# P·V matmuls of an attention kernel issued as three pairs in every third step instead of one pair in each

## The chip, the cores and the metric

The kernel runs on one core of a Trainium2 chip. Its engines work side by side, each with a queue of its own in program order: TensorE (PE, with its weight loader PEld), VectorE (DVE), ScalarE (ACT), GpSimd (POOL), and SyncE (SP), which only issues transfers. The metric is the device time of one execution in microseconds (us); the kernel before takes 831.34 us, the median of three runs (831.29 to 833.1).

## The reference

Attention with a hashing mask (a query sees the keys of its own hash bucket), and two expert layers behind it. Cut to what is computed:

```python
q_bits = (einsum('bhsd,dk->bhsk', q, proj) > 0)          # k_bits likewise, 6 bits each
mask = q_bucket[:, :, :, None] == k_bucket[:, :, None, :]  # bucket = number made of the bits
scores = where(mask, q @ k.T / sqrt(64), -1e9)
attn = exp(scores - max(scores)); attn = attn / (attn.sum(-1) + 1e-9)
x = attn @ v                                              # heads side by side: 1536 x 512
h = x @ w_in;  x = (h - tanh(h)) @ w_out                  # 512 -> 2048 -> 512
out = (silu(x @ w_gate) * (x @ w_val)) @ w_out2           # 512 -> 1536 -> 512
```

Batch 2, 8 heads, sequence 768, head size 64; activations are float32, the weights come as float64.

## The kernel before, in words

**Stages.** The attention stage runs to about 265 us, the two expert layers from there to the end. The order of all instructions on all queues is the order in which the Python code emits them.

**Steps.** The heads are taken in pairs (8 pairs over both batches). A pair has 12 steps: 2 halves of the queries (384 each) × 2 heads `e` × 3 query tiles of 128. That makes 96 steps. The loop at line 529 emits, in iteration `i`:

- `emit_qk(i)` (line 276): the scores of step i, four matmuls into the PSUM tile `s` (two buffers);
- `emit_t(i - 3)` (line 310): six transposes of the probabilities of step i − 3 into the PSUM tile `t`, of which there is one buffer (`ps_t`, line 65), and the copy of `t` into `pt` by ACT (line 323);
- the P·V part (lines 534 to 539), below;
- matmuls that prepare the next pair of heads (`pe[i]`): `hash_mm` at offset 0 of the pair's 12 steps, one one-hot matmul (line 189) at offsets 2, 4, 6 and 8;
- `emit_soft(i)` (line 290): the row maximum `m` on DVE, then the exponential on ACT, which reads `s` and writes `p`;
- `emit_norm(i - 1)` (line 301): two small operations on DVE, then the multiplication of `p` by the reciprocal on POOL;
- other preparation for the next pair (`late + ot[i]`): compares and splits on DVE, ACT (line 204, at offsets 2 to 5) and POOL, and transfers. In the last pair of heads, which has no next one, the first weight chunks are converted instead (three DVE operations, lines 96, 102 and 107, one in each step).

**P·V.** `emit_pv(n, half, kt)` (line 321) issues one pair: for both heads of the pair the matmul of V's 128 keys `kt` (64 columns wide, each head in its own half of the array's columns) with the transposed probabilities. Six pairs, `kt` 0 to 5, add up to one PSUM tile `x`; after the sixth ACT copies it to `xh` (line 345), and the operation `xl` on DVE (line 346) is put into `late`. When the last transposes of a half are emitted, its six pairs join the list `pv` one iteration later (line 537), at i = 9, 15, 21, ... The loop then takes one of them per iteration. Iterations 96 to 107 have no scores; there the expert layers' first matmuls (`a1_mm`, line 358) are emitted too.

Of the kernel before, what the change touches and what calls it, by code (L numbers as in the profile page):

```python
# [30 lines left out]
LAG = 3  # L31
WA, WB = 6, 8
PRE = 6


def chunk_keys():
# [19 lines left out]
def lsh_attention_moe_kernel(ctx: ExitStack, tc: tile.TileContext, qT, kT, vP, proj, cst, wts, out):  # L56
# [25 lines left out]
    def load_next():  # L82
        if n_load[0] < len(keys):
            raw = raw_p.tile([128, 512], I64, tag="raw", name="raw")
            nc.sync.dma_start(out=raw, in_=wts[n_load[0]])
            raws[n_load[0]] = raw
            n_load[0] += 1

    def conv_op(c, step):
        """One of the three integer operations that turn float64 bits into float32 bits."""  # L90
        w = raws[c].bitcast(U32).rearrange("p (n t) -> p n t", t=2)
        lo32, hi32 = w[:, :, 0], w[:, :, 1]
        if step == 0:
            f = raw_p.tile([128, 512], U32, tag="f", name="f")
            cw[c] = f
            nc.vector.tensor_scalar(  # L96
                out=f, in0=hi32, scalar1=3, scalar2=0x3FFFFFF8,
                op0=ALU.logical_shift_left, op1=ALU.bitwise_and,
            )
        elif step == 1:  # L100
            f = cw[c]
            nc.vector.scalar_tensor_tensor(  # L102
                out=f, in0=lo32, scalar=29, in1=f, op0=ALU.logical_shift_right, op1=ALU.bitwise_or
            )
        else:
            f = cw[c]
            nc.vector.scalar_tensor_tensor(  # L107
                out=f, in0=hi32, scalar=0xC0000000, in1=f, op0=ALU.bitwise_and, op1=ALU.bitwise_or
            )
            raws.pop(c)  # L110
            load_next()

    def conv_split(c):
        pool, tag = (wa, "wa") if c % (WA + WB) < WA else (pool_b[0], "wb")
        dst = pool.tile([128, 2, 512], F32R, tag=tag, name=tag)
        ff = cw.pop(c).bitcast(F32)
        nc.scalar.activation(out=dst[:, 0, :], in_=ff, func=ACTF.Copy)
        nc.gpsimd.tensor_tensor(out=dst[:, 1, :], in0=ff, in1=dst[:, 0, :].bitcast(F32), op=ALU.subtract)  # L118
        wgt[keys[c]] = dst

    def conv_slot():
        """One stage of the weights' conversion: split the chunk before, convert the next."""
        if n_split[0] < n_conv[0]:
            conv_split(n_split[0])
            n_split[0] += 1
        if n_conv[0] < len(keys) and live[0] < WA + WB:
            for step in range(3):
                conv_op(n_conv[0], step)
            n_conv[0] += 1
            live[0] += 1  # L130
# [3 lines left out]
    with tc.manual_schedule():  # L134
        nc.scalar.dma_start(out=pj, in_=proj)

        with ExitStack() as at:
# [8 lines left out]
            yin, vin, ldin, bits = {}, {}, {}, {}  # L146
            aq, bq, ak, bk = {}, {}, {}, {}

            def load_y(n):
                t = y_p.tile([128, 2, S], F32, tag="y", name="y")  # L150
                nc.sync.dma_start(out=t[:, 0, :], in_=qT[n * 128:(n + 1) * 128, :])
                nc.sync.dma_start(out=t[:, 1, :], in_=kT[n * 128:(n + 1) * 128, :])
                yin[n] = t
# [6 lines left out]
            def load_h(n, src, nm, eng=nc.sync, heads=(0, 1)):  # L160
                for e in heads:
                    r0 = (2 * n + e) * 64
                    t = ld_p.tile([128, S], F32, tag=nm, name=nm)
                    eng.dma_start(out=t[0:64, :], in_=src[r0:r0 + 64, :])
                    eng.dma_start(out=t[64:128, :], in_=src[r0:r0 + 64, :])
                    ldin[n, e, nm] = t
# [78 lines left out]
            ot = {k: [] for k in range(-12, 12 * len(pairs) + 24)}  # L245

            def prep(n):
                """The pair's preparation, by step: PE work and other work."""
                def put(d, k, f, *a):
                    d[12 * (n - 1) + k].append(lambda: f(n, *a))  # L250

                put(pe, 0, hash_mm)
                put(ot, 1, hash_bits)
                for i, (side, half) in enumerate(((1, 0), (1, 1), (0, 0), (0, 1))):
                    put(pe, 2 + 2 * i, oh_mm, side, half)
                    for e in range(2):
                        put(ot, 2 + 2 * i + e, oh_cmp, side, half, e)
                for i, (e, half) in enumerate(((0, 0), (1, 0), (0, 1), (1, 1))):
                    put(ot, i, hi_a, e, half, "k")
                    put(ot, (4, 4, 5, 6)[i], k_lo, e, half)  # L260
                    put(ot, (5, 7, 9, 10)[i], hi_a, e, half, "q")
                    put(ot, (7, 8, 10, 11)[i], hi_b, e, half)
                    put(ot, (10, 11, 12, 14)[i], q_lo, e, half)
                if n + 1 < len(pairs):
                    put(ot, 0, lambda n: load_y(n + 1))
                    put(ot, 7, lambda n: load_h(n + 1, kT, "k"))
                    put(ot, 14, lambda n: load_h(n + 1, qT, "q"))
                put(ot, 8, load_v)
# [32 lines left out]
            def emit_norm(i):  # L301
                p, sm = pp[i], rr.pop(i)
                r = st_p.tile([128, 1], F32, tag="r", name="r")
                nc.vector.tensor_scalar(out=r, in0=sm, scalar1=1e-9, scalar2=None, op0=ALU.add)
                nc.vector.reciprocal(out=r, in_=r)  # L305
                nc.gpsimd.tensor_scalar(out=p, in0=p, scalar1=r, scalar2=1.0, op0=ALU.mult, op1=ALU.mult)  # L306
# [21 lines left out]
            def emit_pv(n, half, kt):  # L328
                if kt == 0:
                    pool, tag = (ps_h, "h") if (n, half) == (len(pairs) - 1, 1) else (ps_x, "x")  # L330
                    xps[0] = pool.tile([128, TB], F32, tag=tag, name="x")
                x = xps[0]
                for e in range(2):
                    r = slice(64 * e, 64 * e + 64)
                    nc.tensor.matmul(  # L335
                        out=x[r, :], lhsT=vin[n][:, kt, r], rhs=pt[n, half, e][:, kt, :],
                        start=(kt == 0), stop=(kt == NKT - 1), tile_position=(0, 64 * e),
                    )
                if kt == NKT - 1:
                    b, p = pairs[n]  # L340
                    tb = 2 * b + half
                    if p == 0:
                        xh[tb] = xp.tile([128, KT, TB], F32R, tag="xh", name="xh")
                        xl[tb] = xp.tile([128, KT, TB], F32R, tag="xl", name="xl")
                    nc.scalar.activation(out=xh[tb][:, p, :], in_=x, func=ACTF.Copy)
                    late.append(lambda: nc.vector.tensor_tensor(
                        out=xl[tb][:, p, :], in0=x, in1=xh[tb][:, p, :].bitcast(F32), op=ALU.subtract
                    ))
# [134 lines left out]
                f, *a = moe.pop(0)  # L483
                f(*a)

            # the first pair: what its first step needs comes first
            load_y(0)
            load_h(0, kT, "k", nc.scalar)
            load_h(0, qT, "q")
# [36 lines left out]
            pv = []  # L526
            nsteps = len(steps)
            conv0 = nsteps - 12
            for i in range(nsteps + 2 * PRE):
                if i < nsteps:  # L530
                    emit_qk(i)
                if LAG <= i < nsteps + LAG:
                    emit_t(i - LAG)
                if LAG < i <= nsteps + LAG:
                    n2, half2, e2, qt2 = steps[i - LAG - 1]
                    if e2 == 1 and qt2 == 2:
                        pv += [(n2, half2, kt) for kt in range(NKT)]
                if pv:
                    emit_pv(*pv.pop(0))
                for f in pe[i]:  # L540
                    f()
                if i < nsteps:
                    emit_soft(i)
                if 1 <= i <= nsteps:
                    emit_norm(i - 1)
                for f in late + ot[i]:
                    f()
                late.clear()
                c, step = divmod(i - conv0, 3)
                if 0 <= c < PRE:  # L550
                    if step == 0 and c:
                        conv_split(c - 1)
                    conv_op(c, step)
                elif c == PRE and step == 0:
                    conv_split(PRE - 1)
                if i == nsteps:
                    a1_mm(0, 0, 0)
                elif i == nsteps + LAG - 1:
                    emit_moe()
                elif i == nsteps + LAG:  # L560
                    a1_mm(0, 0, 1)
            assert not pv and not late
            n_conv[0] = n_split[0] = live[0] = PRE

# [64 lines left out]
```

## Time and profile before

| what | value |
|---|---|
| median of 3 runs | 831.34 us |
| span of the profiled execution, first to last instruction | 829.2 us |
| PE busy | 810.4 us, 98% of the span |
| PEld busy | 704.2 us, 85% |
| DVE, ACT, POOL busy | 495.0, 340.4, 401.8 us |
| granted TensorE clock, mean | 1.000 of full speed |

The page gives the profiled execution's span, not its whole time; the median of the runs lies 2.1 us above that span. Busy time of PE is the time in which at least one matmul is under way, with modelled ends. "Idle before" is the time an engine had nothing under way before an instruction, and the name behind the arrow is what ended it; "issue" means that nothing in the profile released it.

### The profile page before, as it was taken

To read this page: it belongs to the slowest core of one execution; us is meant where nothing else is said; L and a number is where in the kernel's file an instruction comes from. 1 tells how busy PE (TensorE), PEld (TensorE's weight loads), DVE (VectorE), ACT (ScalarE), POOL (GpSimd) and SP (SyncE) were. 2 spreads that over 40 slices of the span, in tenths; PEclk is the share of its full clock that TensorE was granted. 3 is DMA by queue.
4 is the path that set the end of the run, shared out by engine and by line. 5 is a ranking of instruction groups with operands and counts; after the bars stand their busy time and mean duration, and the time that the engine had idled before them with its cause. 6 is when DMAs were issued, how large, how long until landed. Compare 5 with 4: busy or idle time off the path is not lost.

```text
span 829.2 us, 11946 instructions
## 1 busy us (share of the span) xinstructions
PE 810.4 (98%) x4560; PEld 704.2 (85%) x4560; DVE 495.0 (60%) x807; ACT 340.4 (41%) x610; POOL 401.8 (48%) x404
## 2 busy tenths in 40 slices
PE   5999999999999999999999999999999999999998
PEld 2766666666667999999999998999999999999996
DVE  5777777777784885475376367246835663572222
ACT  2887887788783432232233134222312221221110
POOL 4766766666663773363165177334623441351110
PEclk9999999999999999999999999999999999999999
DMA  8533243231022331121022023002402120210012
GB/s 249 161 96 98 74 119 93 90 102 39 20 78 79 121 130 51 46 100 59 27 92 87 0 102 102 1 26 82 148 1 77 55 98 4 74 51 1 1 39 114
DMA packets 20344, 61.93 MB, mean 75 GB/s; under 512 B 2800, under 2 KB 2800, under 8 KB 20288
## 3 DMA queue, kind: packets, MB, share of 16 engines
q1 hardware_dynamic: 19712, 60.04, 22.0%
q10 hardware_dynamic: 464, 0.80, 0.4%
q8 instruction: 36, 0.59, 0.3%
q0 software_dynamic: 112, 0.33, 0.2%
q14 instruction: 20, 0.16, 0.1%
HBM read 58.02 MB, written 3.15 MB: 74 GB/s over the span
## 4 chain that ended last, share of the span: by engine, by line
PE 92%; DVE 3%; ACT 1%; issue 1%; DMA 1%; POOL 1%; ACTq 0%; POOLq 0%; DVEq 0%
PE pa L358 38%; PE pb L423 15%; PE pb L453 12%; PE s L282 9%; PE x L335 9%; PE t L318 7%; DMA k<-in_kT 1%; PE hps L189 1%; PE hps L174 1%; DVE f L102 1%; DVE f L96 0%; POOL glo L368 0%; DVE th L384 0%; DVE m L293 0%; POOL wb L118 0%
## 5 line engine op out<-in xcount | busy, mean ns | idle before, releaser
L368 POOL TENSOR_TENSOR glo<-u,ghi 128x384 fp32r<-128x384 f32 x48 | 52.8, 1099 | 179.2 <-ACT ghi L367 147.0
L306 POOL TENSOR_SCALAR p<-p,r 128x768 f32<-128x768 f32 x96 | 96.4, 1004 | 71.0 <-DVE r L305 39.8
L368 POOL TENSOR_TENSOR glo<-th,ghi 128x384 fp32r<-128x384 f32 x64 | 76.4, 1214 | 104.0 <-ACT ghi L367 104.0
L358 PE MATMUL pa<-x2h,wb 128*128 128x384 f32 x448 | 116.7, 335 | 1.9 <-DVE u L397 1.9
L293 DVE TENSOR_REDUCE m<-s 128x1 f32<-128x768 f32 x96 | 91.7, 955 | 34.8 <-PE s L282 33.5
L323 ACT ACTIVATE pt<-t 128x768 f32<-128x768 f32 x96 | 77.6, 808 | 43.8 <-PE t L318 42.9
L296 ACT ACTIVATE p<-s,m 128x768 f32<-128x768 f32 x96 | 86.2, 898 | 11.7 <-DVE m L293 9.1
L396 DVE TENSOR_TENSOR u<-pa,u 128x384 f32<-128x384 f32 x48 | 26.7, 556 | 106.1 <-ACT u L395 106.1
L358 PEld LDWEIGHTS pa<-x2h,wb 128*128 128x128 f32 x448 | 81.1, 188 | 2.5 <-DVE u L397 2.2
L358 PE MATMUL pa<-x2h,wa 128*128 128x384 f32 x320 | 83.2, 334 | 0.0
L335 PE MATMUL x<-pt,v 128*64 128x384 f32 x384 | 82.3, 510 | 0.0
L395 ACT ACTIVATE u<-pa 128x384 f32<-128x384 f32 x48 | 23.6, 492 | 139.0 <-PE pa L358 137.6
L318 PE MATMUL t<-csb,p 128*128 128x128 f32 x576 | 79.7, 275 | 0.9 <-ACT pt L323 0.7
L107 DVE SCALAR_TENSOR_TENSOR f<-raw,f 128x512 uint32<-128x512 uint32 x68 | 77.6, 1141 | 2.2
L318 PEld LDWEIGHTS t<-csb,p 128*128 128x128 f32 x576 | 69.1, 142 | 6.9 <-issue 2.5
L358 PE MATMUL pa<-x2l,wb 128*128 128x384 f32 x224 | 74.9, 334 | 0.0
L423 PE MATMUL pb<-ghi,wa 128*128 128x384 f32 x256 | 70.7, 334 | 0.0
L423 PE MATMUL pb<-ghi,wb 128*128 128x384 f32 x256 | 70.7, 334 | 0.0
L282 PEld LDWEIGHTS s<-aqk 128*128 128x128 f32 x192 | 31.3, 196 | 43.4 <-issue 27.3
L358 PE MATMUL pa<-xh,wa 128*128 128x384 f32 x256 | 66.9, 336 | 1.0 <-DVE th L384 1.0
L358 PE MATMUL pa<-xh,wb 128*128 128x384 f32 x256 | 66.2, 334 | 0.0
L282 PE MATMUL s<-aqk 128*128 128x384 f32 x192 | 62.2, 406 | 2.3 <-DVE aqk L232 1.5
(75 smaller groups left out, 1677.4 us busy)
## 6 DMA issues: line engine op xcount, KB each, us to landing
raw<-in_w SPq DMA_DIRECT2D x68, 512.0 KB, 3.2
q<-in_qT SPq DMA_DIRECT2D x32, 192.0 KB, 4.4
k<-in_kT SPq DMA_DIRECT2D x28, 192.0 KB, 3.2
y<-in_qT SPq DMA_DIRECT2D x8, 384.0 KB, 3.2
y<-in_kT SPq DMA_DIRECT2D x8, 384.0 KB, 4.5
v<-in_v SPq DMA_DIRECT2D x8, 384.0 KB, 3.2
out<-acc SPq DMA_DIRECT2D x4, 512.0 KB, 2.8
out<-acc SPq DMA_DIRECT2D x4, 256.0 KB, 2.0
```

Source lines behind the costliest of these rows:

```text
L107: nc.vector.scalar_tensor_tensor(out=f, in0=hi32, scalar=0xC0000000, in1=f, op0=ALU.bitwise_and, op1=ALU.bitwise_or)
L282: nc.tensor.matmul(out=s[:, kh, 0:TB], lhsT=a[n, e, half][:, q0], rhs=b_[n, e, kh], start=first, stop=not first,)
L293: nc.vector.tensor_reduce(out=m, in_=s, axis=AX.XY, op=ALU.max, negate=True)
L296: nc.scalar.activation(out=p.rearrange("p (a b) -> p a b", a=2), in_=s, func=ACTF.Exp, bias=m, accum_out=sm)
L306: nc.gpsimd.tensor_scalar(out=p, in0=p, scalar1=r, scalar2=1.0, op0=ALU.mult, op1=ALU.mult)
L318: nc.tensor.transpose(out=t[:, kt // 3, c0:c0 + 128], in_=p[:, kt * 128:(kt + 1) * 128], identity=ident)
L323: nc.scalar.activation(out=dst, in_=src, func=ACTF.Copy)
L335: nc.tensor.matmul(out=x[r, :], lhsT=vin[n][:, kt, r], rhs=pt[n, half, e][:, kt, :], start=(kt == 0), stop=(kt == NKT - 1), tile_position= ...
L358: nc.tensor.matmul(out=ps, lhsT=w[:, wi, kt * 128:(kt + 1) * 128], rhs=(xh, xl)[xi][tb][:, kt, :], start=(n == 0), stop=(n == 3 * KT - 1),)
L368: nc.gpsimd.tensor_tensor(out=lo, in0=src, in1=hi.bitcast(F32), op=ALU.subtract)
L423: nc.tensor.matmul(out=ps[:, d, 0:TB], lhsT=w[:, wi, dt * 128:(dt + 1) * 128], rhs=gt[xi], start=(n == 0), stop=(n == 3 * G1 - 1),)
L453: nc.tensor.matmul(out=ps[:, d, :], lhsT=u[xi][:, t], rhs=w[:, wi, :], start=(n == 0), stop=(n == 3 * G2 - 1),)
```

## The change

Iterations whose number is a multiple of 3 take up to three pairs from the list, the others none. Line numbers below the new constant are higher by one. (The diff also takes away comments.)

```diff
+PVB = 3
...
-                if pv:
-                    emit_pv(*pv.pop(0))
+                if i % PVB == 0:
+                    for _ in range(min(PVB, len(pv))):
+                        emit_pv(*pv.pop(0))
```

On PE, from the transposes of iteration 9 on, the instructions before stand so (`t` are transposes, `x` the P·V matmuls, `s` the scores):

```order
L318 MATMUL t<-csb,p 128x128 x6
L335 MATMUL x<-pt,v 64x384 x2
L282 MATMUL s<-aqk 128x384 x2
L282 MATMUL s<-bqk 128x384 x2
L318 MATMUL t<-csb,p 128x128 x6
L335 MATMUL x<-pt,v 64x384 x2
L282 MATMUL s<-aqk 128x384 x2
L282 MATMUL s<-bqk 128x384 x2
L318 MATMUL t<-csb,p 128x128 x6
L335 MATMUL x<-pt,v 64x384 x2
L282 MATMUL s<-aqk 128x384 x2
L282 MATMUL s<-bqk 128x384 x2
```

and after the change so:

```order
L319 MATMUL t<-csb,p 128x128 x6
L336 MATMUL x<-pt,v 64x384 x6
L283 MATMUL s<-aqk 128x384 x2
L283 MATMUL s<-bqk 128x384 x2
L319 MATMUL t<-csb,p 128x128 x6
L283 MATMUL s<-aqk 128x384 x2
L283 MATMUL s<-bqk 128x384 x2
L319 MATMUL t<-csb,p 128x128 x6
L283 MATMUL s<-aqk 128x384 x2
L283 MATMUL s<-bqk 128x384 x2
L319 MATMUL t<-csb,p 128x128 x6
L336 MATMUL x<-pt,v 64x384 x6
```

The two matmuls of a pair that stood between the transposes and the next scores in each step are now six in one step, and in the next two steps scores follow directly on transposes.

On ACT, from the copy of iteration 12 on, there stand before (`p` is the exponential, `xh` the first half of the P·V result, `bqk` preparation):

```order
L323 ACTIVATE pt<-t 128x6x128
L296 ACTIVATE p,sm<-s,m 128x768
L323 ACTIVATE pt<-t 128x6x128
L296 ACTIVATE p,sm<-s,m 128x768
L323 ACTIVATE pt<-t 128x6x128
L345 ACTIVATE xh<-x 128x384
L296 ACTIVATE p,sm<-s,m 128x768
L204 ACTIVATE bqk<-hps,csb 64x384
```

and after:

```order
L324 ACTIVATE pt<-t 128x6x128
L346 ACTIVATE xh<-x 128x384
L297 ACTIVATE p,sm<-s,m 128x768
L324 ACTIVATE pt<-t 128x6x128
L297 ACTIVATE p,sm<-s,m 128x768
L324 ACTIVATE pt<-t 128x6x128
L297 ACTIVATE p,sm<-s,m 128x768
L205 ACTIVATE bqk<-hps,csb 64x384
```

`xh` has moved two steps forward, from iteration 14 (offset 2) to iteration 12 (offset 0), in front of that iteration's exponential; the rest keeps its order. In the second half of a pair of heads it moves from offset 8 to offset 6 in the same way.

## Rows read from the trace of the kernel before

**Rows 1.** From the windows view: one stretch of the attention stage, 36 to 218 us. Columns: the stretch, its length, busy us (and number of instructions) of PE, PEld, DVE, ACT and POOL, the granted clock as a share of full speed, the DMA share, GB/s.

```profile
36.00:218.00 182.00, 182.00 (x1118) 118.50 (x1118) 135.87 (x306) 145.82 (x261) 122.18 (x163) 1.00 0.29 85
```

**Rows 2.** From the timeline of PE in one attention step and the start of the next. Columns: start in us, us, engine, line, operation, out<-in, shapes, count. Merged rows can overlap, since matmuls are pipelined. A row of two `s` matmuls (`s<-bqk`) after each `s<-aqk` row is left out.

```profile
96.16 0.62 PE L282 MATMUL s<-aqk 128*128 128x384 f32 x2
...
96.98 0.82 PE L318 MATMUL t<-csb,p 128*128 128x128 f32 x6
97.72 0.87 PE L335 MATMUL x<-pt,v 128*64 128x384 f32 x4
98.52 0.62 PE L282 MATMUL s<-aqk 128*128 128x384 f32 x2
...
99.33 0.82 PE L318 MATMUL t<-csb,p 128*128 128x128 f32 x6
```

**Rows 3.** From the timeline of PEld, PE's weight loader, over the same step; in brackets the idle time before a row and what ended it.

```profile
97.72 0.20 PEld L335 LDWEIGHTS x<-pt,v 128*64 128x64 f32 x4 [0.17 <-issue]
98.52 0.30 PEld L282 LDWEIGHTS s<-aqk 128*128 128x128 f32 x2 [0.60 <-issue]
98.81 0.36 PEld L282 LDWEIGHTS s<-bqk 128*128 128x128 f32 x2
99.15 0.75 PEld L318 LDWEIGHTS t<-csb,p 128*128 128x128 f32 x6
```

**Rows 4.** From the timeline of ACT over the same step.

```profile
97.83 0.81 ACT L323 ACTIVATE pt<-t 128x768 f32<-128x768 f32 x1 [0.43 <-PE t L318]
98.53 0.90 ACT L296 ACTIVATE p<-s,m 128x768 f32<-128x768 f32 x1
```

**Rows 5.** From the timeline of all engines at the end of the attention stage (rows of PE and ACT).

```profile
245.32 0.81 PE L318 MATMUL t<-csb,p 128*128 128x128 f32 x6
...
246.17 0.81 ACT L323 ACTIVATE pt<-t 128x768 f32<-128x768 f32 x1 [0.54 <-PE t L318]
...
247.12 0.84 PE L318 MATMUL t<-csb,p 128*128 128x128 f32 x6 [0.20 <-ACT pt L323]
...
252.99 0.81 PE L318 MATMUL t<-csb,p 128*128 128x128 f32 x6
...
254.80 0.85 PE L318 MATMUL t<-csb,p 128*128 128x128 f32 x6 [0.20 <-ACT pt L323]
...
261.72 3.45 PE L335 MATMUL x<-pt,v 128*64 128x384 f32 x20
```

**Rows 6.** From the timeline of all engines in the steps before the first P·V pair (rows of PE and ACT).

```profile
32.22 0.85 PE L318 MATMUL t<-csb,p 128*128 128x128 f32 x6
...
33.10 0.81 ACT L323 ACTIVATE pt<-t 128x768 f32<-128x768 f32 x1
...
34.06 0.85 PE L318 MATMUL t<-csb,p 128*128 128x128 f32 x6
...
34.94 0.81 ACT L323 ACTIVATE pt<-t 128x768 f32<-128x768 f32 x1
...
35.90 0.85 PE L318 MATMUL t<-csb,p 128*128 128x128 f32 x6
```

**Rows 7.** From the timeline of PE around a step with a one-hot matmul (line 189, issued at 93.73).

```profile
92.19 0.82 PE L318 MATMUL t<-csb,p 128*128 128x128 f32 x6
...
93.77 0.65 PE L282 MATMUL s<-aqk 128*128 128x384 f32 x2
...
94.61 0.82 PE L318 MATMUL t<-csb,p 128*128 128x128 f32 x6
```

**Rows 8.** From the timeline of ACT in the steps with `bqk` work (line 204).

```profile
82.33 0.90 ACT L296 ACTIVATE p<-s,m 128x768 f32<-128x768 f32 x1 [0.32 <-DVE m L293]
...
83.94 0.81 ACT L323 ACTIVATE pt<-t 128x768 f32<-128x768 f32 x1
...
85.67 0.56 ACT L204 ACTIVATE bqk<-hps,csb 64x384 fp32r<-64x384 f32 x1
86.13 0.80 ACT L323 ACTIVATE pt<-t 128x768 f32<-128x768 f32 x1
```

**Rows 9.** From the timeline of DVE: three row maxima (`m`), and the small operations behind the last of them.

```profile
81.27 0.96 DVE L293 TENSOR_REDUCE m<-s 128x1 f32<-128x768 f32 x1
...
95.37 0.94 DVE L293 TENSOR_REDUCE m<-s 128x1 f32<-128x768 f32 x1
...
99.53 0.96 DVE L293 TENSOR_REDUCE m<-s 128x1 f32<-128x768 f32 x1 [0.48 <-PE s L282]
100.40 0.14 DVE L304 TENSOR_SCALAR r<-sm 128x1 f32<-128x1 f32 x1
100.58 0.16 DVE L305 RECIPROCAL r<-r 128x1 f32<-128x1 f32 x1
100.77 0.65 DVE L232 SCALAR_TENSOR_TENSOR aqk<-q,aqk 64x384 fp32r<-64x384 f32 x1
```

**Rows 10.** From the timeline of all engines in the last pair of heads (two rows of DVE, the middle operation of the weights' conversion).

```profile
237.22 1.28 DVE L102 SCALAR_TENSOR_TENSOR f<-raw,f 128x512 uint32<-128x512 uint32 x1
...
244.28 1.68 DVE L102 SCALAR_TENSOR_TENSOR f<-raw,f 128x512 uint32<-128x512 uint32 x1
```

**Rows 11.** From the groups of instructions by line with shapes kept apart: the loads of the P·V weights. Columns: line, engine, operation, out<-in, shapes, count | busy us, mean ns of one | idle us before them and what ended it.

```profile
L335 PEld LDWEIGHTS x<-pt,v 128*64 128x64 f32 x384 | 19.6, 135 | 17.4 <-issue 17.1 <-DMA k<-in_kT 0.2
```

## The prediction

> **What bounds the kernel now.** I read the busy line and the windows first, then the timeline of TensorE (PE) in the attention stage, then that of ScalarE (ACT) beside it, and last the two places where the kernel before already runs attention steps without a P·V pair. The reader is to see in [rows 1] that PE is busy in every one of the 182 us from 36 to 218, at a granted clock of 1.00, while ACT is busy for 146 of them, DVE for 136 and POOL for 122. So in this stage PE's instruction stream sets the pace, and the other three have a fifth to a third of the time to spare. One step in [rows 2] is: scores `s` (from 96.16), six transposes `t` (96.98), one P·V pair `x` (97.72), then the scores of the next step at 98.52. From transposes to transposes (96.98 to 99.33) that is 2.35 us, from scores to scores 2.36; I use 2.355, so 7.07 for three steps.
>
> Two details matter. First, PE's weight loader stands for 0.17 us before the pair's loads and for 0.60 after them [rows 3], so a pair that stands alone occupies PE from 97.72 to 98.52, 0.80 us. Second, the transposes write one PSUM tile, `t`, of which there is a single buffer. ACT empties it with the copy `pt`: it starts 0.85 after the first transpose (96.98 to 97.83 in [rows 2, 4]) and takes 0.81. In the full step it ends at 98.64, while PE is in the next scores, and the next transposes come only at 99.33: the copy has 0.69 us of cover, and the pair's 0.80 us are that cover.
>
> **What the change does to a step.** The same 192 P·V matmuls are issued, with the same operands. Steps with number 0 modulo 3 now issue three pairs and the others none. From step 9 to step 95 that makes 29 threes: one long and two short steps.
>
> *Long step.* What does a pair cost behind another pair? The end of attention shows it: five pairs in a row last 3.45 us, where one pair lasts 0.87 (97.72 in [rows 2], 261.72 in [rows 5]); (3.45 − 0.87)/4 = 0.645 for each further pair. The long step is therefore 2.355 + 2 × 0.645 = 3.645, against 2.355 + 2 × 0.80 = 3.955 if the pairs had kept their price.
>
> *Short step.* PE alone could do it in about 1.40: in [rows 3] the scores' and the transposes' weight loads run without a break from 98.52 to 99.90. But now nothing stands between one step's transposes and the next scores, and the next transposes need `t` empty: 0.85 to 0.88 until the copy starts, 0.81 for it, 0.14 to hand over, 1.80 to 1.84 in all. This is not only a sum. [Rows 6] are the steps of the kernel before that have no pair yet: transposes at 32.22, 34.06 and 35.90, 1.84 apart twice, with the copy 0.88 behind each. [Rows 5] have transposes at 245.32 and 247.12, 1.80 apart with no scores between, and PE idle until "ACT pt". I take 1.81 for the first short step (its copy starts unhindered) and 1.84 for the second (its transposes were themselves held up).
>
> The Trainium skill (Trace Analysis, Matmuls) asks that independent matmul groups rotate through PSUM banks so that the emptying of one runs beside the next group. The trace agrees: with one `t` the idle row at 247.12 names the copy as releaser. By that rule the short step is bounded by the copy's loop, which is what the rows gave.
>
> **The sum.**
> 1. Threes: 3.645 + 1.81 + 1.84 = 7.295 against 7.065, +0.23 each, × 29 = +6.7. Bounds: +0.18 with 1.80 twice, +0.26 if the long step too starts 0.03 late.
> 2. One-hot matmuls (line 189). They lengthen a step from 2.355 to 2.42 (92.19 to 94.61 in [rows 7]), 0.06, four per pair of heads. Three of the four (offsets 2, 4, 8 of 12) now fall in short steps, where PE waits for ACT anyway: −0.06 × 3 × 6 pairs = −1.1.
> 3. ACT's `bqk` work (line 204, offsets 2 to 5). Where it stands in the queue, copies follow one another at 2.19 (83.94 to 86.13 in [rows 8], with `bqk` at 85.67 between); in a 2.36 step that is covered, in a 1.84 step not. A late copy costs only where another set of transposes follows without pairs between; that is so for the `bqk` at offset 4: +0.35 × 6 = +2.1, between 0 and 2.4.
> 4. Evacuation of P·V (`xh` on ACT, `xl` on DVE). It now comes at offsets 0 and 6 instead of 2 and 8. At 6 the chain xh, xl, one-hot compare holds DVE as it did at 8: there the reduction came at 95.37, 1.60 behind its scores at 93.77 (scores in [rows 7], reduction in [rows 9]; a normal one is 1.01 behind, 98.52 to 99.53). An exponential that waits for its reduction follows it after 1.06 (81.27 in [rows 9] to 82.33 in [rows 8]), so 2.66 behind the scores instead of 2.37 (96.16 to 98.53 in [rows 2, 4]). The copy queued behind it on ACT is late by that 0.27 to 0.3, and the transposes after it: +0.27 × 6 = +1.6, between 0 and twice that.
> 5. Weight conversion in the last pair of heads. Its middle operation takes 1.28 to 1.68 us on DVE [rows 10] and falls in the first short step. With a reduction (0.96) and two small operations (0.14 and 0.16, both in [rows 9]) that is over 2.5 us in a 1.81 step. Some of the 0.7 is caught up in the long step: +1.0 for four threes, between 0 and 3.
> 6. End. In the kernel before, the pairs of steps 97 and 98 stand inside the copy's loop (transposes at 252.99 and 254.80 in [rows 5], 1.81 apart), and cost nothing. Now they are issued in step 96, ahead of it: 2 × 0.645 = +1.3. The last six pairs wait for the last copy as they did.
>
> Together 6.7 − 1.1 + 2.1 + 1.6 + 1.0 + 1.3 = +11.6. The profiled execution's span is 829.2; 829.2 + 11.6 = 840.8. The median of the runs, 831.34, lies 2.1 above the span, so 842.9; I write 842.5. With every term at its lower or upper bound the case runs from +5.7 to +17, 837 to 848. The expert stage behind attention is only shifted: its instructions and their order are the same. P·V results come two steps earlier, but their first readers come long after.
>
> **Rivals.**
> *Fewer switches win (faster).* If the short step ran at PE's own 1.40, a three would be 3.645 + 2.80 = 6.445, −0.62, × 29 = −18; with +1.3 at the end and 2.1 outside the span about 815. It decides where the copy's loop is shorter than 1.71, the short step at which a three costs what it cost before. For it: the 0.17 and 0.60 us of standing loader around each lone pair [rows 3], two thirds of which go. Against it: 1.84, 1.84, 1.80 and 1.81 in [rows 5, 6].
>
> The Trainium skill (TensorEngine Tiling (Array Packing), Key Properties) says that changing the tiling mode drains TensorE; the pairs run on 64-column tiles, the rest on the full array. The trace agrees in [rows 3]; by that rule alone the time would be that of this rival.
>
> *The two sides cancel (no change).* Needs a mean short step of 1.71, for instance if the copy follows the transposes 0.1 sooner when its engine is idle, or if terms 3 to 5 come to nothing and the switch is dearer than the loader shows. About 831. [Rows 6] show the copy 0.88 behind its transposes, at 34.94, and none sooner than 0.85, so I give it little.
>
> *The queues lock together (much slower).* In a short step DVE has 0.96 + 0.30 + one preparing operation of about 0.65 [rows 9], 1.9 us in 1.84, and ACT, with `bqk` in its queue, 2.19 [rows 8]. If the lag isn't made good in the long step, every short step runs at 2.19: a three takes 3.645 + 4.38 = 8.025, +0.96, × 29 = +28, and with the end and the 2.1 outside the span about 860. Against it: the long step leaves each of these engines over 1.5 us, twice the lag of two short steps.
>
> **How the numbers follow.** Forecast 0.66; fewer switches win 0.13; cancel 0.12; locked queues 0.09. About 0.3% (2.5 us) is what a measurement of this kernel can tell from no change. Faster takes the first rival and a little of the second, 0.14; same takes the rest of the second, and a little of the forecast's low end, 0.12; slower the remainder, 0.74. The range has to leave out two in ten: it leaves out the faster rival and the far end of the locked queues, and reaches from 829.5 (cancel) to 852 (a third of the way from the forecast's upper end to 860). The forecast's own range is 837 to 848.
>
> **What would show it.** In the profile of the changed kernel, transposes to transposes should read 3.65, 1.81, 1.84 in turn; the first transposes of most short steps should be idle before, released by "ACT pt", some 0.4 us each, 20 to 25 us in all; the loader's idle time before the pairs, 17.4 us in [rows 11], should fall to about a third; offsets 4 to 6 should show a step near 2.2. If PE's idle time in the attention stage stays near nothing, the forecast is wrong and the first rival right. If "PE s" or "DVE m" waits grow over 10 us, the queues lock.

## The result, and the profile after

The changed kernel takes 843.33 us (median of 4 runs, 842.47 to 843.84) against 832.22 for the kernel before in the same comparison: a ratio of 1.0133, 95% interval 1.012 to 1.0145. It is slower by about 11 us. Its profiled execution has a span of 841.1 us, 11.9 more than before.

The page's busy line of the changed kernel first, then the window of its attention stage (columns as in [rows 1]):

```profile
PE 809.2 (96%) x4560; PEld 704.4 (84%) x4560; DVE 494.7 (59%) x807; ACT 340.2 (40%) x610; POOL 400.2 (48%) x404
```

```profile
36.00:226.00 190.00, 181.89 (x1123) 119.65 (x1122) 135.49 (x307) 146.04 (x262) 121.58 (x163) 1.00 0.28 83
```

PE has done the same work in 1 us less of busy time and 12 us more of span. In [rows 1] every microsecond of the stage was covered; now 190 us have 181.9 of them, at a granted clock of 1.00 as before.

One long and two short steps in the timeline of PE, which answer to [rows 2]:

```profile
97.65 0.84 PE L319 MATMUL t<-csb,p 128*128 128x128 f32 x6
98.43 2.16 PE L336 MATMUL x<-pt,v 128*64 128x384 f32 x12
100.51 0.61 PE L283 MATMUL s<-aqk 128*128 128x384 f32 x2
...
101.32 0.82 PE L319 MATMUL t<-csb,p 128*128 128x128 f32 x6
...
103.12 0.84 PE L319 MATMUL t<-csb,p 128*128 128x128 f32 x6 [0.29 <-ACT pt L324]
...
104.96 0.85 PE L319 MATMUL t<-csb,p 128*128 128x128 f32 x6
```

The pairs are one block of 12 records (98.43), and in the two steps behind it scores (left out here, but for 100.51) and transposes follow one another. From transposes to transposes: 97.65 to 101.32 is 3.67, to 103.12 is 1.80, to 104.96 is 1.84. PE stood 0.29 before the transposes at 103.12, until "ACT pt".

The timeline of ACT beside it, which answers to [rows 4]:

```profile
102.17 0.81 ACT L324 ACTIVATE pt<-t 128x768 f32<-128x768 f32 x1 [1.73 <-PE t L319]
...
104.01 0.81 ACT L324 ACTIVATE pt<-t 128x768 f32<-128x768 f32 x1
```

The copy at 102.17 starts 0.85 after its transposes and ends at 102.98; the next transposes follow at 103.12, 0.14 later. The copy at 104.01 is 0.89 behind its transposes, ends at 104.82, and the transposes follow at 104.96. So one step's pace is now the way round `t`: transposes, copy, transposes.

The offsets 4 to 7 of a pair of heads in the timeline of PE, and two rows of ACT in it:

```profile
116.73 0.82 PE L319 MATMUL t<-csb,p 128*128 128x128 f32 x6
...
118.55 0.84 PE L319 MATMUL t<-csb,p 128*128 128x128 f32 x6
...
120.72 0.85 PE L319 MATMUL t<-csb,p 128*128 128x128 f32 x6 [0.27 <-ACT pt L324]
...
124.47 0.81 PE L319 MATMUL t<-csb,p 128*128 128x128 f32 x6
```

```profile
119.32 0.56 ACT L205 ACTIVATE bqk<-hps,csb 64x384 fp32r<-64x384 f32 x1
119.78 0.79 ACT L324 ACTIVATE pt<-t 128x768 f32<-128x768 f32 x1
```

Here 116.73 to 118.55 is 1.82, but 118.55 to 120.72 is 2.17: the copy stands behind `bqk` and starts at 119.78, 1.23 after its transposes. The long step behind it takes 3.75, with a one-hot matmul in it.

Groups by line (columns as in [rows 11], to which the last one answers), two of the kernel before first:

```profile
L318 PE MATMUL t<-csb,p 128*128 128x128 f32 x576 | 79.7, 275 | 0.9 <-ACT pt L323 0.7
...
L282 PEld LDWEIGHTS s<-aqk 128*128 128x128 f32 x192 | 31.3, 196 | 43.4 <-issue 27.3 <-ACT bqk L204 7.2 <-ACT pt L323 3.8
```

```profile
L319 PE MATMUL t<-csb,p 128*128 128x128 f32 x576 | 81.1, 277 | 11.2 <-ACT pt L324 8.7
...
L283 PEld LDWEIGHTS s<-aqk 128*128 128x128 f32 x192 | 30.6, 195 | 28.7 <-ACT p L297 17.7 <-issue 4.8 <-ACT xh L346 3.8
...
L336 PEld LDWEIGHTS x<-pt,v 128*64 128x64 f32 x384 | 24.9, 136 | 29.2 <-issue 28.2 <-ACT pt L324 0.8 <-DMA k<-in_kT 0.2
```

PE's waiting shows before its transposes: 11.2 us where it was 0.9. The loader's idle time is not PE's. Before the scores it has fallen from 43.4 to 28.7 us; of the 17.7 for the exponential a part is 0.60 each behind a run of pairs, which stood behind each lone pair before ([rows 3]); only the rest is new, and stands in short steps. Before the pairs it has risen from 17.1 to 28.2.

Where the 11.9 us of span came from, measured between the same transposes in the two timelines of PE:

| stretch (first transposes of the step) | before | after | difference |
|---|---|---|---|
| start to step 6 | 35.90 | 36.71 | +0.81 |
| step 6 to step 81 (25 threes) | 183.18 | 190.19 | +7.01 |
| step 81 to step 92 (last pair of heads) | 26.24 | 28.09 | +1.85 |
| step 92 to step 95 | 9.48 | 10.79 | +1.31 |
| step 95 to the end | 574.4 | 575.3 | +0.9 |

The first row isn't the change's: the instructions up to there stand in the same order, and the constants arrived later in that execution. (In pvb2, pvb6 and bqk5 below, with the same instructions up to there, step 6 stands at 35.88, 36.92 and 36.75.) The last row comes from the start of the expert layers, from this stretch of the timeline (ACT, POOL and DVE):

```profile
276.18 0.49 ACT L346 ACTIVATE xh<-x 128x384 fp32r<-128x384 f32 x1 [5.51 <-PE x L336]
276.56 0.62 ACT L118 ACTIVATE wa<-f 128x512 fp32r<-128x512 f32 x1
...
277.27 1.47 POOL L119 TENSOR_TENSOR wa<-f,wa 128x512 fp32r<-128x512 f32 x1 [3.49 <-ACT wa L118]
...
277.63 1.66 DVE L103 SCALAR_TENSOR_TENSOR f<-raw,f 128x512 uint32<-128x512 uint32 x1
```

The same operation on DVE in the kernel before:

```profile
266.66 0.69 DVE L102 SCALAR_TENSOR_TENSOR f<-raw,f 128x512 uint32<-128x512 uint32 x1
```

The middle operation of the weights' conversion took 1.66 us beside a subtraction on POOL; in the kernel before it took 0.69, and the subtraction wasn't beside it. What hangs on it is 0.9 late, and that stays to the end. This does come from the change: with the last three pairs in iteration 102 the last `xh` stands in front of the last `wa` in ACT's queue, where before it stood behind it (`wa` at 261.56, `xh` at 265.21), and the subtraction on POOL waits for `wa`. In the traces of all runs below the operation takes 1.65 to 1.67 in every kernel with three or six pairs per run, and 0.69 to 0.70 in every kernel with one or two, whose last pair comes in iteration 104, behind `wa`.

### The profile page after: what moved, and what is told of

Same layout as the page of the kernel before. It is cut to its first block, busy times and chain, and to the rows that moved or that the text cites. A ratio compares the mean times of both kernels' runs of the same rounds, so it can differ in the third digit from the quotient of the medians.

```text
span 841.1 us, 11941 instructions
## 1 busy us (share of the span) xinstructions
PE 809.2 (96%) x4560; PEld 704.4 (84%) x4560; DVE 494.7 (59%) x807; ACT 340.2 (40%) x610; POOL 400.2 (48%) x404
## 4 chain that ended last, share of the span: by engine, by line
PE 86%; ACT 5%; DVE 4%; issue 2%; POOL 1%; DMA 1%; ACTq 0%; POOLq 0%; DVEq 0%
PE pa L359 37%; PE pb L424 15%; PE pb L454 12%; PE x L336 8%; PE t L319 7%; PE s L283 6%; ACT pt L324 3%; ACT p L297 1%; DMA k<-in_kT 1%; DVE f L103 1%; PE hps L190 1%; PE hps L175 1%; DVE m L294 1%; DVE f L97 1%; POOL glo L369 0%
## 5 line engine op out<-in xcount | busy, mean ns | idle before, releaser
L307 POOL TENSOR_SCALAR p<-p,r 128x768 f32<-128x768 f32 x96 | 94.5, 984 | 79.6 <-DVE r L306 45.6
L319 PE MATMUL t<-csb,p 128*128 128x128 f32 x576 | 81.1, 277 | 11.2 <-ACT pt L324 8.7
L319 PEld LDWEIGHTS t<-csb,p 128*128 128x128 f32 x576 | 64.4, 142 | 29.8 <-issue 18.5
L336 PE MATMUL x<-pt,v 128*64 128x384 f32 x384 | 69.8, 495 | 0.1
L385 DVE TENSOR_TENSOR th<-pa,th 128x768 f32<-128x768 f32 x32 | 30.6, 956 | 57.9 <-ACT th L384 57.9
```

Of the source, the lines that this page charges most:

```text
L319: nc.tensor.transpose(out=t[:, kt // 3, c0:c0 + 128], in_=p[:, kt * 128:(kt + 1) * 128], identity=ident)
L336: nc.tensor.matmul(out=x[r, :], lhsT=vin[n][:, kt, r], rhs=pt[n, half, e][:, kt, :], start=(kt == 0), stop=(kt == NKT - 1), tile_position= ...
```

## The experiments

The theory: a step without pairs is bounded by the loop transposes, copy, transposes over the one buffer of `t`, and the loss grows with the number of such steps. Its rivals: the run of six P·V matmuls itself costs the time; the moved evacuation or ACT's total work does; or a saving of switches wins in some other grouping. Unless said otherwise, edits are made to the changed kernel; every run has its ratio to the kernel before on the same chip.

### Two pairs in every second step, six in every sixth

```diff
-PVB = 3
+PVB = 2
```

> Two pairs in every second step. Theory (a lone transpose-copy-transpose loop of 1.81 to 1.84 us per step without pairs, 0.645 us per further pair): long step 2.355 + 0.645 + 0.025 = 3.03, short step 1.81, so 4.84 for two steps against 4.71 before, +0.13 x 43 = +5.6; the one-hot matmuls all fall in long steps and save nothing, no late copy from the bqk work since a long step follows every short one; +0.65 at the end of attention. Together about +6 to +8: 838 to 840 with a base of 832, and the transposes 3.03 and 1.81 apart in turn. Rival (the loss comes with the later terms, bqk and evacuation, not with the loop): no more than +2. Rival (switches win once the run is short): below 830.

Measured: 838.58 us, ratio 1.0076 (1.0059 to 1.0093). The transposes in its timeline of PE:

```profile
96.22 0.81 PE L319 MATMUL t<-csb,p 128*128 128x128 f32 x6
...
98.03 0.84 PE L319 MATMUL t<-csb,p 128*128 128x128 f32 x6 [0.17 <-ACT pt L324]
...
101.07 0.82 PE L319 MATMUL t<-csb,p 128*128 128x128 f32 x6
...
102.87 0.85 PE L319 MATMUL t<-csb,p 128*128 128x128 f32 x6 [0.29 <-ACT pt L324]
```

1.81, 3.04, 1.80: each long step as worked out, and every second step at the loop's pace.

```diff
-PVB = 3
+PVB = 6
```

> Six pairs in every sixth step. Theory: long step 2.355 + 5 x 0.645 + 0.025 = 5.605, then 1.81 and four times 1.84, 14.78 against 14.13 for six steps, +0.65 x 14 = +9; the bqk work at offsets 2, 3 and 4 now each makes a copy late, 3 x 0.35 x 6 pairs = +6; two of three of the saved one-hot times as with three, -1; +3.2 at the end of attention less about 1 that the last pairs no longer wait; conversion +2. Together +17 to +20: 849 to 852. Rival (a loss per run of pairs, not per step without pairs): fewer runs, so less than with three, under +11.

Measured: 852.67 us, ratio 1.0251 (1.0231 to 1.0271), just above the 849 to 852 expected. The transposes of offsets 1 to 7:

```profile
111.73 0.82 PE L319 MATMUL t<-csb,p 128*128 128x128 f32 x6
...
113.54 0.85 PE L319 MATMUL t<-csb,p 128*128 128x128 f32 x6 [0.30 <-ACT pt L324]
...
115.38 0.84 PE L319 MATMUL t<-csb,p 128*128 128x128 f32 x6
...
117.41 0.85 PE L319 MATMUL t<-csb,p 128*128 128x128 f32 x6 [0.28 <-ACT pt L324]
...
119.73 0.85 PE L319 MATMUL t<-csb,p 128*128 128x128 f32 x6
...
121.90 0.85 PE L319 MATMUL t<-csb,p 128*128 128x128 f32 x6 [0.28 <-ACT pt L324]
...
127.57 0.82 PE L319 MATMUL t<-csb,p 128*128 128x128 f32 x6
```

1.81, 1.84, 2.03, 2.32, 2.17, then 5.67 for the long step. The steps beside `bqk` are slow for more steps now, as there is no long step between them. One pair per step, two, three and six give 832, 839, 843 and 853: fewer runs of pairs cost more, which leaves no room for a price per run.

### Half of the copy

The copy takes three of the six blocks, and the P·V matmuls read these three twice: half of the probabilities are left out, PE's work is the same.

```diff
-                dst = pt[n, half, e][:, :, qt * 128:(qt + 1) * 128].rearrange("p (a c) q -> p a c q", a=2)
-                src = t[:, :, 0:TB].rearrange("p a (c q) -> p a c q", c=3)
+                dst = pt[n, half, e][:, 0:3, qt * 128:(qt + 1) * 128]
+                src = t[:, 0, 0:TB].rearrange("p (c q) -> p c q", c=3)
...
-                    out=x[r, :], lhsT=vin[n][:, kt, r], rhs=pt[n, half, e][:, kt, :],
+                    out=x[r, :], lhsT=vin[n][:, kt, r], rhs=pt[n, half, e][:, kt % 3, :],
```

With three pairs in every third step:

> Three pairs in every third step, but the copy of the transposes takes only the first three of the six blocks, and the P.V matmuls of the key blocks 3 to 5 read blocks 0 to 2 instead: half of the probabilities are left out of the result, PE does the same number of matmuls. Theory: the copy takes 0.49 instead of 0.81 and can start after three transposes, the loop is 1.15 to 1.5, so a step without pairs runs at PE's own 1.40 to 1.5; a three takes 3.67 + 2.8 to 3.0 = 6.5 to 6.7 against 7.07, -0.4 to -0.6 x 29: 815 to 822, at least 10 us below half1. Rival (the run of six P.V matmuls or the earlier evacuation costs the time, not the copy): the same +11 over half1, about 843.

With one pair in each step (`PVB = 1`):

> One pair in every step as before, with the same shortened copy (half of the probabilities left out in the same way). Theory: the copy was covered by the pair, so its length doesn't matter: 831 to 833, transposes 2.35 to 2.36 apart. Rival (ACT's total work bounds the stage): several us faster than before.

Measured: 828.12 us (ratio 0.9955, 0.994 to 0.997) with three pairs, 830.08 (0.9977, 0.9966 to 0.9987) with one. Transposes of both, the three-pair kernel first:

```profile
96.53 0.82 PE L319 MATMUL t<-csb,p 128*128 128x128 f32 x6
...
98.02 0.85 PE L319 MATMUL t<-csb,p 128*128 128x128 f32 x6
...
99.65 0.82 PE L319 MATMUL t<-csb,p 128*128 128x128 f32 x6
```

```profile
97.83 0.82 PE L319 MATMUL t<-csb,p 128*128 128x128 f32 x6
...
100.19 0.81 PE L319 MATMUL t<-csb,p 128*128 128x128 f32 x6
```

A shorter copy takes 15 us from the changed kernel and turns its sign, and leaves the steps with one pair at 2.36. The 1.5 us that half1 gained lie before step 6 (34.46 against 35.90), where steps have no pair yet (the two in front of step 6 take 1.49 and 1.61 in place of 1.84 each); between steps 6 and 81 it takes 183.15 us, as before. So the copy was covered before the change and is bare after it: that is shown.

The size was a miss: 815 to 822 was expected, at least 10 us below half1, and it is 2 below. The first short step takes 1.49 (96.53 to 98.02), since the copy still starts 0.88 after its first transposes and not after three of them; the second takes 1.63. This is what it waits for, in the waits of PEld between 36 and 215 us (total us, times, longest):

```profile
PEld s L283 <- ACT p L297: 15.3, 37, 0.6
```

Of the 37, 12 are the loader's 0.60 behind a run of pairs; the other 25, some 8 us, stand in short steps. So behind the loop over `t` lies a second one, over the two buffers of `s`: scores wait for the exponential of two steps before. It costs most at offset 9 (90.84 to 92.89, 2.05), where the evacuation makes the exponential late (91.03, behind a reduction at 90.00); in the changed kernel the longer copy hides that.

### Two copies

To keep the whole computation, the transposes were emptied by two copies of 384 columns, each issued behind its three transposes. A first form kept one tile for the stage:

```diff
-                t = ps_t.tile([128, 2, 512], F32, tag="t", name="t")
+                t = tt[0]
...
+                for a in range(2):
+                    for c in range(3):
...
+                    dst = pt[n, half, e][:, 3 * a:3 * a + 3, qt * 128:(qt + 1) * 128]
+                    src = t[:, a, 0:TB].rearrange("p (c q) -> p c q", c=3)
+                    nc.scalar.activation(out=dst, in_=src, func=ACTF.Copy)
```

> One pair in each step as before, the transposes' tile held for the whole stage and emptied by two copies of 384 columns, each issued behind its three transposes (complete computation). Theory: with the pair as cover the copy doesn't bound, so nothing moves: 830 to 833, although ACT has one more instruction per step (0.49 + 0.49 in place of 0.81). Rival (ACT's work bounds): several us slower.

> Two pairs in every second step with the same two copies. Theory: the loop falls from 1.81 to 1.24 (second half's copy ends 1.43 after the first transpose, 0.14 to hand over, its successor comes 0.33 into the next transposes), so the short step runs at PE's 1.40 to 1.5: 3.03 + 1.45 = 4.48 against 4.71, -0.23 x 43 = -10: 821 to 823 if nothing else binds; in half3 a second loop, scores waiting for the exponential of two steps before, bound the short steps at 1.6 to 2.0 in part, and with it 823 to 829. Below before in any case. Rival (the added copy makes ACT the bound): 832 or more.

> Three pairs in every third step with the same two copies. Theory: first short step 1.40 to 1.5, second one bound by ACT (two copies and an exponential, 1.75 to 1.9) and by scores that wait for the exponential: a three 6.9 to 7.1 against 7.07, bqk and evacuation offsets late as in half3: 828 to 836, between half3 and the changed kernel, and slower than split2. Rival (batching itself costs): 843 as the changed kernel.

Measured: 909.79, 917.10 and 914.45 us (ratios 1.094, 1.102, 1.100). All three missed, by 77 to 88 us. The timeline of PE in split1:

```profile
103.05 0.49 PE L321 MATMUL t<-csb,p 128*128 128x128 f32 x3
104.12 0.55 PE L321 MATMUL t<-csb,p 128*128 128x128 f32 x3 [0.58 <-ACT pt L326]
```

The second three transposes (104.12) come 1.07 after the first three (103.05), 0.33 being their own length, and the row names "ACT pt": they wait for the copy of the first half, although they write the other half of the tile. So in this form the copy stands inside every step, bare whatever the grouping, and the three kernels differ by under 1%. As a trial of the loop it failed; but it priced a copy without cover: 78 us in 96 steps, 0.8 us each, about the 0.74 by which these transposes are late.

The second form gives each half a tile of its own, from a pool that lives for the attention stage:

```diff
+            ps_a[0] = at.enter_context(tc.tile_pool(name="ps_a", bufs=1, space=PSUM))
...
+                for a in range(2):
+                    t = ps_a[0].tile([128, 512], F32, tag=("ta", "tb")[a], name="t")
...
```

> One pair in each step as before, the transposes in two PSUM tiles of one bank each, each emptied by its own copy of 384 columns (complete computation). In split1 to split3 both halves lay in one tile, and the second three transposes waited for the first half's copy within the step, which cost all three the same. Theory: with two tiles that wait is gone and the pair covers the copies: 830 to 834. Rival (two copies per step are too much for ACT): above 836.

> Two pairs in every second step, transposes in two tiles. Theory: the copy's loop is 1.24 to 1.3, the short step runs at PE's 1.40 to 1.5, a two takes 4.45 to 4.55 against 4.71, -0.16 to -0.26 x 43: 821 to 826, up to 829 if scores wait for exponentials as in half3; below before in any case. Rival (added ACT work makes ACT the bound): 832 or more.

> Three pairs in every third step, transposes in two tiles. Theory: first short step 1.40 to 1.5, second bound by ACT (two copies, an exponential and its sum, 1.75 to 1.9): a three 6.9 to 7.1 against 7.07; 826 to 836, clearly below the changed kernel's 843 and not below two2. Rival (batching itself costs): 843.

Measured: 831.19 us (ratio 0.9991, 0.9981 to 1.0001), 824.34 (0.9905, 0.9886 to 0.9925) and 829.73 (0.9977, 0.9967 to 0.9987). The timeline of PE with two pairs in every second step:

```profile
101.91 0.82 PE L321 MATMUL t<-csb,p 128*128 128x128 f32 x6
...
103.26 0.82 PE L321 MATMUL t<-csb,p 128*128 128x128 f32 x6
...
106.34 0.82 PE L321 MATMUL t<-csb,p 128*128 128x128 f32 x6
```

This short step takes 1.35 (101.91 to 103.26), with no idle time of PE; the six of a pair of heads take 1.35 to 1.79. With one pair a step the two tiles change nothing; with two pairs the kernel is faster than both the kernel before and the changed one. With three pairs a wait for the exponential is left in the second short step:

```profile
97.51 0.82 PE L321 MATMUL t<-csb,p 128*128 128x128 f32 x6
98.49 0.62 PE L284 MATMUL s<-aqk 128*128 128x384 f32 x2 [0.16 <-ACT p L298]
...
99.29 0.82 PE L321 MATMUL t<-csb,p 128*128 128x128 f32 x6
```

Scores stand 0.16 for "ACT p", and the step takes 1.78 (97.51 to 99.29).

### One `bqk` operation moved

```diff
-                        put(ot, 2 + 2 * i + e, oh_cmp, side, half, e)
+                        put(ot, 2 + 2 * i + (e if i != 1 else 1), oh_cmp, side, half, e)
```

> The changed kernel with one of ACT's four bqk operations per pair of heads moved from offset 4 to offset 5, where a long step follows. Theory (term 3: the one at offset 4 makes the copy and the transposes behind it 0.34 to 0.35 late, in six pairs of heads): the step at offset 6 falls from 2.18 to 1.84, -2.0 us, about 841.3, ratio to before 1.010 to 1.011. Rival (ACT's queue is late there for another reason, or the lateness moves to the next step): no change from the changed kernel's 1.0133.

Measured: 842.19 us, ratio 1.0117 (1.010 to 1.0135). The transposes of offsets 5 to 7:

```profile
117.94 0.85 PE L319 MATMUL t<-csb,p 128*128 128x128 f32 x6
...
119.79 0.85 PE L319 MATMUL t<-csb,p 128*128 128x128 f32 x6
...
123.54 0.82 PE L319 MATMUL t<-csb,p 128*128 128x128 f32 x6
```

117.94 to 119.79 is 1.85 in place of 2.17, and the long step behind it is 3.75 as before, so the lateness doesn't move on. From step 6 to step 81 this kernel takes 188.16 us against 190.19, −2.03. The ratio's interval contains the changed kernel's 1.0133, so by time alone it is inconclusive; the timeline settles it.

## Why the prediction was right, point by point

The forecast, 842.5, came within 1 us of the 843.33, and the mechanism is the one it named.

- *Long step.* Forecast 3.645, measured 3.67: two further pairs cost 0.64 each, as the five pairs at the end had shown, and 0.03 comes from the transposes in front having been held up, which was given as a bound.
- *Short steps.* 1.81 and 1.84 forecast, the same measured. The steps of the kernel before that had no pair yet had already told it. A three takes 7.32, +0.255 against 7.065 where the sum had +0.23. The last of the 29 costs more: in the kernel before, its third step had no scores any more and already stood at 1.80 ([rows 5], 245.32 to 247.12), so it was 6.52 and not 7.065, and is 7.34 now. Term 1 counted it as +0.23; it is +0.8.
- *One-hot matmuls.* Three of four are hidden, as said; the fourth costs 0.08. About −1.0 against −1.1.
- *`bqk`.* Forecast +0.35 at offset 6, measured 0.33 to 0.34, and bqk5 took it away: shown.
- *Evacuation.* Term 4 failed: +1.6 was forecast and the step that should carry it, at offset 9, takes 1.84. Two rows of ACT show why, beside transposes at 95.81:

```profile
95.79 0.90 ACT L297 ACTIVATE p<-s,m 128x768 f32<-128x768 f32 x1
...
96.69 0.81 ACT L324 ACTIVATE pt<-t 128x768 f32<-128x768 f32 x1
```

The exponential is as late as worked out (95.79, behind a reduction at 94.76), but the copy behind it starts at 96.69, 0.88 after its transposes, as in any short step. The step that failed is "the copy queued behind it on ACT is late by that 0.27": in a short step without evacuation ACT is idle for 0.23 between exponential and copy (102.88 + 0.90 to 104.01), and the lateness ends there.

- Terms 1 to 4 for the 25 threes up to step 81: 6.4 − 1.0 + 2.0 + 0 = 7.4 against 7.01 measured.
- *Weight conversion.* Term 5 was too high. The last pair of heads lost 1.85. Three threes account for 0.8; the long and the short step behind them, which end the stretch, take 5.51 against 4.72, another 0.8. About 0.3 is left for the conversion and the evacuation beside it, forecast 1.0: two short steps are late, by 0.35 (2.19) and 0.24 (2.05), but in the kernel before one step was late already, by 0.28 (2.64, 228.51 to 231.15).
- *End.* +1.3 forecast, +1.31 measured.
- *Expert layers.* "The expert stage behind attention is only shifted: its instructions and their order are the same" failed too: the order of `xh` and `wa` on ACT changed at its start, and cost the 0.9 of the table.
- That the total fits so well is in part luck: term 4 was 1.6 and term 5 0.7 too high, and against that the last three was 0.6 too low and the 0.9 in the expert layers and the 0.8 at the start of that execution, which the profiled span has, were not forecast. The stated bounds of the terms add up to +5.4 and +16.3, not to +5.7 and +17; nothing hangs on that.

Two of the signs that were named for the profile came out differently. PE's idle time was to be 20 to 25 us; its row shows 8 to 11, since in the second short step scores wait first, for the exponential (0.18 before their loads at 103.91), and transposes then start without a visible gap. And the loader's idle time before the pairs was to fall to a third; it rose from 17.4 to 29.2. Its timeline over the long step:

```profile
98.42 0.20 PEld L336 LDWEIGHTS x<-pt,v 128*64 128x64 f32 x4 [0.17 <-issue]
98.80 0.14 PEld L336 LDWEIGHTS x<-pt,v 128*64 128x64 f32 x2 [0.18 <-issue]
...
100.51 0.30 PEld L283 LDWEIGHTS s<-aqk 128*128 128x128 f32 x2 [0.60 <-ACT p L297]
...
103.91 0.30 PEld L283 LDWEIGHTS s<-aqk 128*128 128x128 f32 x2 [0.18 <-ACT p L297]
```

The loader stands 0.18 before every two loads inside a run too, twice for each further pair, while PE is busy with the matmuls before. So the 0.17 before a pair, which the prediction took for a sign of the switch, is none; the 0.60 behind stands once per run. What a run saves is 0.36 us for each pair behind its first: a step with one pair takes 2.355 and one without, where nothing holds it, 1.35 (two2), so a lone pair costs 1.00 and a further one in a run 0.64. That fits a price of the switch, but no run separates it from other causes. "Two thirds of the standing loader go" was the wrong sign to look for.

The rival "fewer switches win" had the saving right and the condition too: with the copies split over two tiles the loop falls below PE's pace and batching wins 7 us (two2). The rule that groups should rotate through PSUM banks (the Trainium skill, Perfetto Trace Analysis, Matmuls) is borne out by the same run: the same grouping with one tile is 7 us slower than before (pvb2).

## What to carry to other kernels

Before work is gathered into longer runs, look at what it covers where it stands: here one matmul pair in each step was the time in which another engine emptied a single buffer, and gathering the pairs saved PE 0.7 us in each three steps (7.07 against 3.67 + 2 × 1.35) and bared 0.95 of waiting for the copy. Steps that run without that work somewhere in the same trace (the filling and the emptying of a pipeline) show the price beforehand. Once the buffer was split in two, gathering paid: 7 us with two pairs per run, under 2 with three.

## What the runs showed of the hardware that wasn't expected

The same DVE operation (128x512 uint32, line 102 of the kernel before) took 0.69 us alone and 1.66 us beside a subtraction on POOL, and the place of one copy in ACT's queue went with which of the two it was, in every trace. In runs of pairs on 64-column tiles the loader idles 0.18 us before every two loads, while PE goes on at 0.64 us per pair. And PE's standing for 8 us of 190, at most 0.3 us at a time in the steady steps, left the granted clock at 1.00 of full speed in the attention stage.
